# A causal 7-tap convolution and a GELU feed-forward on one core: four more seven-product blocks, a new channel order, and one operand sum made by transfers

## The chip, the cores and the metric

The kernel runs on one core of a Trainium2 chip. The metric is the device time of one execution in microseconds (us); the figure for a kernel is the median of several runs. The engines of the core are named as in the profile: PE (TensorE, matrix products; PEld is its weight load), DVE (VectorE), ACT (ScalarE), POOL (GpSimd, which here mostly issues transfers) and SP (SyncE, which issues loads and stores). Each engine works through its own instructions in the order in which they were written, and engines wait for one another through semaphores.

## The reference

The first stage is a causal convolution over the sequence with seven taps; each of eight heads has its own softmax-normalised weights, shared by the head's 24 channels. The second is a feed-forward layer with an exact GELU.

```python
batch, seq, d_model = (8, 4096, 192); kernel_size = 7; n_heads = 8
w = softmax(weight, axis=-1)                     # [8, 7]
out[b,s,h,:] = sum_k w[h,k] * x_pad[b, s+k, h, :]  # six rows of zeros ahead of each sequence
h = x @ w_in                                      # [32768,192] @ [192,2048]
g = 0.5 * h * (1.0 + erf(h * inv_sqrt2))
return (g @ w_out).astype(np.float32)             # [32768,2048] @ [2048,192]
```

(The first two lines after the sizes say in short what the reference spells out with padding, indices and an einsum.)

## The kernel before

**Tiling.** The 32768 tokens are cut into two halves that are worked on side by side, one on partitions 0 to 63 and one on partitions 64 to 127. Each half is cut into 35 blocks: six of 256 tokens, then 29 of 512 (`WS`, line 33). The 192 channels are three groups (`NP`) of 64. Before the change, group p holds channels 3r + p, r = 0 to 63, so that each partition r belongs to one head and the convolution weight of a tap is one scalar per partition (`wcol`).

**A block's way.** SP loads x (`load`, line 626, four transfers into `xin`). DVE transposes it in 32x32 squares so that channels lie on partitions (`trans`, line 777, into `xT`). POOL copies the last six columns of the block before ahead of it (`halo`, line 710). The convolution is seven taps (`conv`, line 802): the first is a multiplication, made on ACT for most blocks (`first_tap`, line 933) and on DVE otherwise; the other six are multiply-adds on DVE, the last of which writes `xc` in bf16. PE multiplies by W_in (`mm1`, line 1032) in 16 slots of 12 matmuls into the two `hp` buffers; ACT applies the GELU to each slot (line 974) into `gT`. `gT` and the other block buffers are double, indexed by the block's parity. In the next block's slots, between the pieces of its `mm1`, PE multiplies `gT` by W_out.

**The second product in two forms.** A plain block (N below; `mm2_t`, line 1129) takes 192 matmuls of 512 columns, that is 48 rounds, a round being four matmuls on the four quarters of the array. A seven-product block (S; `mm2_s`, line 1162; the list `ST`, line 72) treats part of the product as a 2x2 block matrix and uses seven products in place of eight, with sums and differences of its operands: 44 rounds. The weight sums are made once (`weights`). Per S block the following are made from `gT`: S1, S3, Dn and S4 (`st_add`, line 549; `st_dma`, line 541). S1, Dn and S4 are written to the tiles `sst`, of which there is one each; S3 is added in place in `gT`. They are made in pieces by k, the eight pairs of hidden chunks: S1 in pieces of 4, 2 and 2, Dn and S4 in halves. Before, the first two pieces of S3 are transfers that add in place, issued by POOL, and the last is a DVE addition. S1 is read by the products P5, E1 and e1, S3 by P7, Dn by P6 and S4 by P3. The order of the products in each quarter is written out by hand (`TILES`, line 388), and `ROUNDS` says how many rounds go into each slot.

**After the products of an S block** ACT copies partial sums out of PSUM (`st_copy`, line 571: p5, p1, e, u, p3, and u with a minus sign twice), DVE combines them (`st_post`, line 600: k0, k3, k4) and transposes them into `osb` (`st_evac`, line 615: ev); SP stores them (`store`, line 638). k0 waits for P7, and k4 for the end of the block's products. A bank of PSUM is handed to the next user by `release` (line 480).

**The order on DVE.** It is the convolution taps, block by block (`plan`), with the sums, combinations and transposes put between them at places listed in `AT_ST` and `at_ev`. On ACT the places of the first taps and of the copies are in `TAPS` and `AT_COPY`. On POOL, halos and transfers follow a loop over blocks (line 743).

**Before block 6** the blocks are prepared in other ways (the first two have their convolution on PE; W_in is loaded by POOL at the start, `win_in`). W_in lies in SBUF in bf16, three rows for the three channel groups on each partition, and for the upper half of the partitions with columns swapped in pairs of 256.

Of the kernel before, what the change touches and what calls it, by code (L numbers as in the profile page):

```python
# [11 lines left out]
def bass_lightweight_conv__then__act_gelu_exact_kernel(  # L12
# [39 lines left out]
    NX = 3  # L52


    DQ = D // 2

# [15 lines left out]
    ST = [m for m in range(M0 + 3, M1) if m % 2 == 1]  # L72
    K0 = {n: i for i, n in enumerate([4, 5, 6, *range(9, NB)])}
# [48 lines left out]
    with es:  # L122
# [61 lines left out]
        S_K0 = sem("S_K0")  # L184
        S_WT = sem("S_WT")
        S_ST = sem("S_ST")
# [3 lines left out]
        S_AD = [sem("S_AD%d" % q) for q in range(2)]  # L190
# [50 lines left out]
        def wait_pc(e, n, p):  # L241
# [11 lines left out]
            n: [(0, 0, 2), (0, 2, 1)] * (n not in K0) + [(k, 0, NP) for k in range(1, KS)]  # L253
            for n in range(NB)
            if n not in PC
        }
        FQ = F // 8
# [55 lines left out]
        def wait_banks(t, m, g):  # L313

            k = G0[m] + g
            if m < M0:
                if k >= 2:
                    t.wait_ge(S_EVA, k - 1)
            elif g % 2:
                t.wait_ge(S_GELU, SL0[NB] - 1 + g // 2)  # L320
            else:
                for b in LAST[g : g + 2]:
                    t.wait_ge(*release(OWNER[b], b))
# [42 lines left out]
        def evac_t(v, m, j):  # L366
# [22 lines left out]
            (0, 0): "P1 D1 e2 e1 D2 P6 P2", (1, 0): "D1 P1 P2 e2 e1 D2 P6",  # L389
            (0, 1): "P5 P7 E2 E1 P4 P3", (1, 1): "E2 P7:2 P5 P7:6 P3 E1 P4",  # L390
# [3 lines left out]
        EVENTS = []  # L394
        for (hf, cg), names in TILES.items():
            at, done = 0.0, {}
            for u in names.split():
                u, k1 = (u.split(":") + ["8"])[:2]
                k0 = done.get(u, 0)
                d = SPAN.get(u, (0, TB))[1] / TB  # L400
                for k in range(k0, min(8, k0 + int(k1))):
                    EVENTS.append((at, hf, cg, u, k))
                    at += d / 8
                    done[u] = k + 1
            assert abs(at - 5.5) < 1e-6 and all(k == 8 for k in done.values())
        EVENTS.sort(key=lambda q: (round(q[0], 4), q[1], q[2]))
        GROUP = {}
        for e, (at, hf, cg, u, k) in enumerate(EVENTS):
            name = {"D": "DE", "E": "DE", "e": "Ea"}.get(u[0], u)
            GROUP[name] = e  # L410
        DONE = {GROUP[name] for name in NE}
        SWITCH, last = {}, {}
        for e, (at, hf, cg, u, k) in enumerate(EVENTS):
            p = last.get((UNIT[u][0], cg))
            if p is not None and EVENTS[p][1] != hf:
                SWITCH[e] = p
                DONE.add(p)
            last[UNIT[u][0], cg] = e
        FIRST = {}
        for e, (at, hf, cg, u, k) in enumerate(EVENTS):  # L420
            FIRST.setdefault((UNIT[u][0], cg), e)
        DONE.discard(len(EVENTS) - 1)
        DONE = sorted(DONE)
        ROUNDS = (3, 3, 2, 3, 3, 2, 3, 3, 2, 4, 3, 3, 2, 3, 3, 2)
        assert sum(ROUNDS) == 44

        def st_done(e, m, name):
            if GROUP[name] == len(EVENTS) - 1:
                e.wait_ge(S_MM2, MMC[m + 1])
            else:  # L430
                e.wait_ge(S_ST, len(DONE) * ST.index(m) + DONE.index(GROUP[name]) + 1)

        COPIES = ("p5", "p1", "e", "u", "p3", "-u", "-g")
        AT_COPY = {
            "p5": (1, 6), "p1": (1, 8), "e": (1, 14), "u": (2, 0), "p3": (2, 2), "-u": (2, 6), "-g": (2, 10),
        }

        def ac(m, name):

            return len(COPIES) * ST.index(m) + COPIES.index(name) + 1  # L440

        POSTS = ("k0", "k3", "k4")

        def dp(m, name):

            return len(POSTS) * ST.index(m) + POSTS.index(name) + 1

        SUMS = {"S1": (0, 4, 6, 8), "S3": (6, 8), "Dn": (0, 4, 8), "S4": (0, 4, 8)}

        def sa(m, name, k):  # L450

            return (len(SUMS[name]) - 1) * ST.index(m) + [k < q for q in SUMS[name][1:]].index(True) + 1

        AT_ST = [
            (2, 1, 0, "S1", 0), (2, 1, 2, "Dn", 0), (2, 1, 4, "S4", 0), (2, 1, 6, "S1", 1),
            (2, 2, 2, "S1", 2), (2, 2, 4, "S3", 0), (2, 3, 0, "Dn", 1), (2, 4, 0, "S4", 1),
            (2, 5, 0, "k0", 0), (3, 1, 0, "ev", 2),
            (3, 6, 0, "k3", 0), (4, 1, 1, "ev", 1), (4, 1, 5, "k4", 0), (4, 2, 0, "ev", 0),
        ]

        def at_ev(n):

            if n == M0:
                return [(3, 1, 3), (3, 2, 1), (3, 2, 3)]
            return [(3, 1, 3), (3, 2, 1), (3, 2, 3)]
# [3 lines left out]
        for n in range(M0, M1):  # L469
            if n not in ST:  # L470
                SIDE += [((n + at[0], *at[1:]), "ev", n, j) for j, at in enumerate(at_ev(n))]
            else:
                SIDE += [((n + d, o, r), name, n, q) for d, o, r, name, q in AT_ST]
        SIDE.sort(key=lambda q: q[0])
        EV = {}
        for _, name, n, j in SIDE:
            if name in ("ev", "evac"):
                EV[n, j] = EVC[M0 - 1] + len(EV) + 1

        def release(m, b):  # L480
# [4 lines left out]
            if k == "X":  # L485
                return S_AC, ac(m, "p3")
# [5 lines left out]
        for m in range(M0, M1):  # L492
            for b in BK[m].values() if m in ST else BK[m]:
                REL[m, b] = release(OWNER[b], b) if b in OWNER else None
                OWNER[b] = m
# [45 lines left out]
        def st_dma(e, m, q):  # L541

            k, k1 = SUMS["S1"][q : q + 2]
            e.wait_ge(S_SA["S1"], sa(m, "S1", k))
            e.dma_start(  # L545
                quad(m, 1, 0, k, k1 - k), quad(m, 0, 0, k, k1 - k), accum_op=ALU.add
            ).then_inc(S_AD[q], 16)

        def st_add(v, m, name, q):
# [7 lines left out]
            v.wait_ge(S_GELU, SL0[m] + 2 * k1)  # L557
            if name == "S1":
                ins = v.tensor_tensor(t("S1"), quad(m, 1, 0, k, n), quad(m, 1, 1, k, n), ALU.add)  # L559
            elif name == "S3":  # L560
                v.wait_ge(S_SA["S1"], sa(m, "S1", k))
                ins = v.tensor_tensor(quad(m, 1, 0, k, n), quad(m, 0, 0, k, n), quad(m, 1, 0, k, n), ALU.add)
            elif name == "Dn":
                v.wait_ge(S_SA["S1"], sa(m, "S1", k1 - 1))
                ins = v.tensor_tensor(t("Dn"), quad(m, 0, 0, k, n), t("S1"), ALU.add)
            else:
                v.wait_ge(S_SA["Dn"], sa(m, "Dn", k1 - 1))
                ins = v.tensor_tensor(t("S4"), quad(m, 0, 1, k, n), t("Dn"), ALU.add)
            ins.then_inc(S_SA[name])

        def st_copy(a, m, name):
# [6 lines left out]
            if name[0] != "-":  # L578
                st_done(a, m, {"p5": "P5", "p1": "P1", "e": "Ea", "p3": "P3", "u": "P6"}[name])
            if name == "e":  # L580
                dst, src = bank(BK[m]["D"], UP, HA), bank(BK[m]["V"], LO, HA)
            else:
                dst, src = {
                    "p5": (p5s[UP, :], xb(UP)),
                    "p1": (gsm[LO, :], xb(LO)),
                    "u": (uu[LO, :], xb(LO)),
                    "-u": (uu[UP, :], uu[LO, :]),
                    "p3": (tq[LO, :], xb(UP)),
                    "-g": (gsm[UP, :], uu[LO, :]),
# [4 lines left out]
            if name == "p1" and i:  # L594
                a.wait_ge(S_EV, EV[ST[i - 1], 0])
            if name == "p3" and i:
                a.wait_ge(S_EV, EV[ST[i - 1], 1])
            a.activation(out=dst, in_=src, func=AF.Copy, scale=-1.0 if name[0] == "-" else 1.0).then_inc(S_AC)

        def st_post(v, m, name):  # L600
            if name == "k0":
                st_done(v, m, "P7")
                v.wait_ge(S_AC, ac(m, "p5"))
                ins = v.tensor_tensor(tq[UP, :], bank(BK[m]["Y"], UP), p5s[UP, :], ALU.subtract)
# [708 lines left out]
```

## Time and profile before

| what | us |
|---|---|
| median of 3 runs (lowest, highest) | 669.04 (668.91, 669.47) |
| the profiled execution | 667.87 |
| its span, first to last instruction | 666.1 |
| DVE convolution taps, line 827 | 282.9 of busy time, 165 instructions, plus 56.7 in 33 last taps |
| ACT gelus, line 974 | 513.0, 510 instructions |
| DVE input transposes, line 800 | 76.2, 39 instructions |
| transfers that add in place, POOL, line 545 | 26, of 512 and 256 KB |

The span is what the profile accounts for; the run's time also has what lies around it. Busy time of an engine is the time in which it had an instruction at work, and a group's mean mixes shapes unless they are told apart. A wait is the idle time of an engine ahead of an instruction, with the instruction elsewhere that ended it. The granted TensorE clock is 1.00 in every stretch. In 40 equal slices the busy tenths of DVE and ACT are 9 in most, and the DMA engines' share is 0.46 to 0.48 in the steady pairs.

### The profile page before, as it was taken

What the parts mean: (1) busy time and instruction counts of PE and PEld (TensorE: products, weight loads), DVE (VectorE), ACT (ScalarE), POOL (GpSimd) and SP (SyncE); (2) the same over time, 40 slices, a digit from 0 to 9 for tenths busy, and PEclk for the clock granted to TensorE, in tenths of its full rate; (3) what the DMA queues carried; (4) which work ended last, traced back from release to release, by engine and by line L of the source; (5) the groups of instructions that cost most, each with busy time, mean ns of one, the idle gap of its engine ahead of it and who ended that gap; (6) DMA issues with size and microseconds to landing.
All of it is one profiled execution on the core that took longest, in us unless ns stands there. A gap on an engine that the chain in (4) does not pass through costs nothing.

```text
span 666.1 us, 27567 instructions
## 1 busy us (share of the span) xinstructions
PE 661.4 (99%) x12712; PEld 516.4 (78%) x12712; DVE 600.7 (90%) x510; ACT 610.8 (92%) x720; POOL 47.6 (7%) x87
## 2 busy tenths in 40 slices
PE   8999999999999999999999999999999999999998
PEld 8999655557667787877878778787787878878787
DVE  6979999799999999999999999999999999999632
ACT  8999988889999999999999999999999999999884
POOL 7000000010000100001010010100001000010100
PEclk9999999999999999999999999999999999999999
DMA  9735334243081461905529073370824719151233
GB/s 159 165 89 130 65 69 97 72 93 79 18 197 29 107 135 34 203 7 127 114 41 201 3 163 78 62 179 2 191 50 91 151 29 192 22 118 29 56 90 97
DMA packets 137028, 63.92 MB, mean 96 GB/s; under 512 B 126800, under 2 KB 133520, under 8 KB 136912
## 3 DMA queue, kind: packets, MB, share of 16 engines
q1 hardware_dynamic: 129136, 49.37, 33.2%
q0 software_dynamic: 6656, 12.19, 10.1%
q8 instruction: 100, 1.64, 1.1%
q10 hardware_dynamic: 1120, 0.59, 0.3%
q14 instruction: 16, 0.13, 0.1%
HBM read 28.31 MB, written 25.17 MB: 80 GB/s over the span
## 4 chain that ended last, share of the span: by engine, by line
PE 99%; ACT 0%; DVE 0%; DMA 0%; issue 0%; ACTq 0%
PE hp L1066 50%; PE ob L1150 23%; PE ob L1202 18%; PE ob L1106 5%; PE ob L1258 1%; PE hp L1258 1%; PE ob L1011 0%; DMA wsb<-in_weight_dram 0%; PE ob L1066 0%; ACT dg L912 0%; DVE wcol L772 0%; ACT xc L237 0%; ACT osb L347 0%; ACT wex L899 0%; ACT xTb L269 0%
## 5 line engine op out<-in xcount | busy, mean ns | idle before, releaser
L974 ACT ACTIVATE gT<-hp 128x1024 bf16<-128x1024 f32 x510 | 513.0, 1022 | 43.0 <-PE hp L1066 35.7
L1066 PE MATMUL hp<-xc,win 64*64 64x512 bf16 (+2 forms) x6036 | 438.4, 366 | 0.2
L1066 PEld LDWEIGHTS hp<-xc,win 64*64 64x64 bf16 (+1 forms) x6036 | 247.2, 106 | 73.0 <-ACT gT L974 4.6
L827 DVE SCALAR_TENSOR_TENSOR acc<-xT,wcol,acc 128x1536 f32<-128x1536 f32 (+1 forms) x165 | 282.9, 1714 | 10.6 <-ACT acc L938 7.3
L1150 PE MATMUL ob<-gT,wot 64*64 64x512 bf16 x2880 | 205.6, 376 | 0.0
L1202 PE MATMUL ob<-gT,wot 64*64 64x512 bf16 x832 | 158.0, 376 | 0.0
L1150 PEld LDWEIGHTS ob<-gT,wot 64*64 64x64 bf16 x2880 | 112.1, 107 | 43.3
L1202 PE MATMUL ob<-gT,wst 64*64 64x512 bf16 (+2 forms) x832 | 144.0, 323 | 0.0
L1202 PE MATMUL ob<-s_S,wot 64*64 64x128 bf16 (+2 forms) x624 | 89.9, 305 | 0.0
L800 DVE STREAM_TRANSPOSE xT<-xin 128x1536 f32<-128x1536 f32 (+2 forms) x39 | 76.2, 1963 | 3.8 <-DMA xin<-in_x_dram 1.4
L1202 PEld LDWEIGHTS ob<-gT,wst 64*64 64x64 bf16 x832 | 68.5, 107 | 10.7
L1202 PEld LDWEIGHTS ob<-gT,wot 64*64 64x64 bf16 x832 | 63.9, 107 | 1.5
L938 ACT ACTIVATE acc<-xT,wcol 128x512 f32<-128x512 f32 (+1 forms) x87 | 61.2, 703 | 0.0
L827 DVE SCALAR_TENSOR_TENSOR xc<-xT,wcol,acc 128x1536 bf16<-128x1536 f32 (+1 forms) x33 | 56.7, 1720 | 0.8
L1202 PE MATMUL ob<-s_S,wst 64*64 64x512 bf16 x208 | 57.4, 376 | 0.0
L1202 PE MATMUL ob<-s_Dn,wst 64*64 64x512 bf16 x208 | 57.4, 376 | 0.0
L1202 PEld LDWEIGHTS ob<-s_S,wot 64*64 64x64 bf16 x624 | 50.2, 107 | 8.6
L545 POOL DMA_DIRECT2D gT<-gT x26 | 22.4, 861 | 318.1 <-DVE s_S L559 318.1
L1106 PE MATMUL ob<-wout,gT 64*128 64x192 bf16 x768 | 41.9, 243 | 0.0
L1106 PEld LDWEIGHTS ob<-wout,gT 64*128 64x128 bf16 x768 | 35.1, 94 | 3.3
L373 DVE STREAM_TRANSPOSE osb<-ob 128x512 f32<-128x512 f32 x45 | 31.1, 694 | 6.2 <-PE ob L1150 6.2
L559 DVE TENSOR_TENSOR s_S<-gT 128x1024 bf16<-128x1024 bf16 (+1 forms) x39 | 32.6, 837 | 1.4 <-ACT gT L974 1.3
(78 smaller groups left out, 322.6 us busy)
## 6 DMA issues: line engine op xcount, KB each, us to landing
out_dram<-osb SPq DMA_DIRECT2D x124, 192.0 KB, 3.6
xin<-in_x_dram SPq DMA_DIRECT2D x116, 192.0 KB, 4.2
gT<-gT POOLq DMA_DIRECT2D x13, 512.0 KB, 4.6
gT<-gT POOLq DMA_DIRECT2D x13, 256.0 KB, 3.3
xin<-in_x_dram SPq DMA_DIRECT2D x18, 96.0 KB, 2.5
wout<-in_moe_w_out_dram POOLq DMA_DIRECT2D x4, 192.0 KB, 4.7
win<-in_moe_w_in_dram POOLq DMA_DIRECT2D x4, 96.0 KB, 4.3
win<-in_moe_w_in_dram POOLq DMA_DIRECT2D x2, 192.0 KB, 4.5
```

What stands on the lines that cost most here:

```text
L373: v.transpose(osb_t(m, j), bank(BK[m][j])).then_inc(S_EV)
L545: e.dma_start(quad(m, 1, 0, k, k1 - k), quad(m, 0, 0, k, k1 - k), accum_op=ALU.add).then_inc(S_AD[q], 16)
L559: ins = v.tensor_tensor(t("S1"), quad(m, 1, 0, k, n), quad(m, 1, 1, k, n), ALU.add)
L800: v.transpose(out, src).then_inc(S_TR)
L827: ins = v.scalar_tensor_tensor(dst, src, wk, a, op0=ALU.mult, op1=ALU.add)
L938: a.activation(out=acc[n % 2][:, p * TB : p * TB + w], in_=ap(xT[n % 2], p * XW + HX, [[NP * XW, 128], [1, w]]), func=AF.Copy, scale=wcol[ ...
L974: a.activation(out=ap(gT[n % 2], (i % 2 * NF + i // 2) * TB if n in ST else i * c * 2 * w, dst), in_=ap(ob, 2 * TB, [[4 * TB, 128], *src[1 ...
L1066: ins = t.matmul(hbuf(u, slice(fo, fo + fw), o, w), ap(win, f1, [[NP * F, 64], [2, fw]]), xc[n % 2][r, p * TB : p * TB + w], start=(p == 0 ...
L1106: ins = t.matmul(bb[sub], gT[m % 2][r, c0 : c0 + 128], wout[r, CH[sub][i] * C : (CH[sub][i] + 1) * C], start=(ph == 0 and k == 0), stop=(p ...
L1150: ins = t.matmul(bank(BK[m][j], slice(64 * h, 64 * h + 64), w), ap(wot, 64 * hf * NF * C + CH[h][i] * C + 64 * j, [[NF * C, 64], [1, 64]]) ...
L1202: ins = t.matmul(bank(BK[m][bk], slice(64 * cg, 64 * cg + 64))[:, c0 : c0 + w], wt_, x, start=(e == mine[0]), stop=(e == mine[-1] or e in ...
L1258: ins = t.matmul(banks(m, g)[h], gT[m % 2][:, c0 : c0 + 128], wout[:, CH[h][i] * C : (CH[h][i] + 1) * C], start=(i == 0), stop=(i == NF - 1),)
```

## The change

1. **Four more seven-product blocks.** `ST` is 9, 10, 12, 13, ... 30, 31, 33: two of three blocks, 17 in place of 13.
2. **Channels in runs of eight from block 7 on.** Group p then holds channels 24h + 8p + j of each head h, j = 0 to 7. The input transpose reads runs of eight adjacent words and no longer single words at a distance of three. W_in's rows must follow: POOL loads it again in place, in four parts (`win_again`), each when block 6 has used its columns, and PE waits for each part in block 7. The halo of block 7 is made from 32 rows of x that SP loads again and DVE transposes in the new order.
3. **Sums.** S3 is wholly made by transfers. In an S block that follows an N block, the first half of Dn is too: a transfer copies `gT` into the tile, and a second adds S1. The products that read S3 stand later in the orders, of which there are now two, for an S block behind an N block and for one behind an S block.
4. **Copies.** p1 and p5 are one ACT copy of all 128 partitions (p15). The tiles `gsm` and `tq` alternate with `p5s` and `wtf` from one S block to the next.
5. **Banks** are handed over by halves of 64 partitions.
6. **Written orders.** From block 9 on DVE follows `LIST`, ACT `SLOT` and POOL `GLIST`, in which each step is named with its block. Blocks 13, 16, 19, 22, 25, 28, 31 and 34 have one third of their first tap on ACT and two thirds on DVE; the other blocks from 9 on have all of it on ACT.

```diff
-    ST = [m for m in range(M0 + 3, M1) if m % 2 == 1]
+    ST = [m for m in [9, 10, 12, 13, 15, 16, 18, 19, 21, 22, 24, 25, 27, 28, 30, 31, 33] if m < M1]
+    LIST = {
...
+        18: "Dn.1.15 ev.2.14 1 S4.1.15 ev.1.13 k0.0.15 2 S1.0.16 3 S1.1.16 4 ev.2.15 5 S1.2.16 Dn.0.16 Dn.1.16 6",
+        19: "S4.0.16 k4.0.15 t19 ev.0.15 0 S4.1.16 k0.0.16 t20 k3.0.15 1 ev.1.15 2 ev.2.16 3 4 5 k4.0.16 6",
+        20: "t21 1 S1.0.18 2 k3.0.16 3 S1.1.18 ev.0.16 4 ev.1.16 ev.0.17 ev.1.17 S1.2.18 ev.2.17 Dn.1.18 5 S4.0.18 S4.1.18 6",
+        21: "1 k0.0.18 2 t22 3 S1.0.19 S1.1.19 ev.2.18 Dn.0.19 4 S1.2.19 S4.0.19 Dn.1.19 5 k4.0.18 6",
...
+        27: "1 k0.0.24 2 t28 S1.0.25 S1.1.25 3 ev.2.24 4 S1.2.25 5 Dn.0.25 Dn.1.25 S4.0.25 k4.0.24 6",
...
+    SLOT = {
...
+        20: "0:p3.18 2:u.18 4:-g.18 6:p15.19 9:-u.18 12:f0.23 13:e.19",
+        21: "0:u.19 2:-g.19 3:p3.19 4:f1.23 6:f2.23 8:-u.19 9:f0.24 11:f1.24",
+        22: "2:f2.24 6:p15.21 12:f2.25 13:e.21",
...
+            "N": {
+                (0, 0): "P1 D1 e1 e2 D2 P6 P2", (1, 0): "D1 P1 P2 e1 e2 D2 P6",
+                (0, 1): "P5 P7:6 E1 P7 E2 P4 P3", (1, 1): "E1:4 E2:4 P7:2 P5 P7:4 P3:2 P7 P3 E2 E1 P4",
+            },
+            "S": {
+                (0, 0): "P1 D1 e2 e1 D2 P6 P2", (1, 0): "D1 P1 P2 e2 e1 D2 P6",
+                (0, 1): "P5 P7:6 E2 P7 E1 P4 P3", (1, 1): "E2 P7:2 P5 P7:4 P3:2 P7 P3 E1 P4",
+            },
...
+        ROUNDS = (3, 3, 2, 3, 3, 2, 4, 2, 2, 4, 3, 3, 2, 3, 3, 2)
...
+        BYDMA = {'N': 'S3.0 S3.1 S3.2 Dn.0', 'S': 'S3.0 S3.1 S3.2'}
...
+        def st_dma(e, m, name, q):
+
+            if name == "S3":
+                k, k1 = SUMS["S3"][q : q + 2]
+                e.wait_ge(*summed(m, "S1", k))
+                e.dma_start(
+                    quad(m, 1, 0, k, k1 - k), quad(m, 0, 0, k, k1 - k), accum_op=ALU.add
+                ).then_inc(S_AD["S3.%d" % q], 16)
+                return
+            k, k1 = SUMS["Dn"][q : q + 2]
+            d, s1 = (ap(sst[x], k * TB, [[NF // 2 * TB, 128], [1, (k1 - k) * TB]]) for x in ("Dn", "S1"))
+            if name == "cp":
+                e.wait_ge(S_GELU, SL0[m] + 2 * k1)
+                st_read(e, m, "Dn", q)
+                if ST.index(m):
+                    e.wait_ge(*summed(ST[ST.index(m) - 1], "S4", k))
+                e.dma_start(d, quad(m, 0, 0, k, k1 - k)).then_inc(S_AD["cp.%d" % q], 16)
+            else:
+                e.wait_ge(S_AD["cp.%d" % q], SUM_AT[m, "Dn", q][1])
+                e.wait_ge(*summed(m, "S1", k1 - 1))
+                e.dma_start(d, s1, accum_op=ALU.add).then_inc(S_AD["Dn.%d" % q], 16)
...
+        GLIST = (
...
+            "cp.0.18 Dn.0.18 S3.0.18 S3.1.18 S3.2.18 halo.22 S3.0.19 S3.1.19 S3.2.19 "
...
+            def win_again(k):
+                g.wait_ge(S_MM1, SL0[NR - 1] + (4, 8, 14, 16)[k])
+                c0 = 2 * FQ * (0, 2, 1, 3)[k]
+                for hf in range(2):
+                    for p in range(NP):
+                        g.dma_start(
+                            ap(win, (64 * hf * NP + p) * F + c0, [[NP * F, 64], [1, 2 * FQ]]),
+                            ap(wint, RUN * p * F + c0, [[GRP * F, 8], [F, RUN], [1, 2 * FQ]]),
+                        ).then_inc(S_WR[k], 16)
...
-                        [[TB // 32 * DQ, 128], [1, NP], [DQ, w // 32], [NP, 32]],
...
+                    if n >= NR:
+                        run = [[RUN, NP], [DQ, w // 32], [GRP, 4], [1, RUN]]
...
+                if n == NR and i in (0, 4, 8, 10):
+                    t.wait_ge(S_WR[(0, 4, 8, 10).index(i)], 32 * NP)
```

In `LIST` a bare number is a tap of the block that heads the line, `t22` the transpose of block 22, and `S1.0.19` the first piece of S1 of block 19. In `SLOT`, `12:f0.23` is the first third of block 23's first tap ahead of slot 12's GELU.

## The prediction

> **What bounds it now.** I read the page's busy shares and the chain that ended last first: the engine order is settled there.
>
> ```profile
> PE 661.4 (99%) x12712; PEld 516.4 (78%) x12712; DVE 600.7 (90%) x510; ACT 610.8 (92%) x720; POOL 47.6 (7%) x87
> ...
> PE 99%; ACT 0%; DVE 0%; DMA 0%; issue 0%; ACTq 0%
> ```
>
> PE is the whole chain; no other engine appears in it after the head. A busy PE need not be PE at its peak, so I took stretches of the steady part, each one pair of blocks (one with seven products, "S", one plain, "N").
>
> ```profile
> core 0: us, PE busy (x) PEld busy (x) DVE busy (x) ACT busy (x) POOL busy (x), PEclk, DMA share, GB/s
> 292.91:333.52 40.61, 40.61 (x791) 32.67 (x786) 39.21 (x32) 38.46 (x46) 2.55 (x4) 1.00 0.48 99
> 333.52:374.13 40.61, 40.61 (x790) 32.66 (x786) 39.21 (x32) 38.46 (x46) 2.55 (x4) 1.00 0.46 100
> ```
>
> A pair is the same 40.61 us every time, PE without a gap, DVE at 39.21 (97%), ACT at 38.46 (95%). In units of four matmuls of 512 columns on the four quarters of the array ("rounds"), a block's first product takes 48 rounds, the second 48 in N and 44 in S: 96 + 92 = 188 rounds, so a round is 40.61 / 188 = 0.2160 us, N takes 20.73 us and S 19.87. PE sets the time, with DVE 1.4 us per pair behind it. The question is therefore whether DVE and the transfers can feed more S blocks. For that I read DVE's groups by form and a piece of its timeline.
>
> ```profile
> L827 DVE SCALAR_TENSOR_TENSOR acc<-xT,wcol,acc 128x1536 f32<-128x1536 f32 x145 | 262.6, 1811 | 6.1 <-ACT acc L938 3.4
> ...
> L800 DVE STREAM_TRANSPOSE xT<-xin 128x1536 f32<-128x1536 f32 x29 | 68.6, 2369 | 2.3
> ...
> L624 DVE STREAM_TRANSPOSE osb<-tq 128x512 f32<-128x512 f32 x13 | 9.1, 702 | 0.0
> ...
> L800 DVE STREAM_TRANSPOSE xT<-xin 128x768 f32<-128x768 f32 x4 | 4.9, 1229 | 1.4 <-DMA xin<-in_x_dram 1.4
> ```
>
> ```profile
> 341.65 1.17 DVE L559 TENSOR_TENSOR s_S<-gT 128x2048 bf16<-128x2048 bf16 x1
> 342.75 0.69 DVE L624 STREAM_TRANSPOSE osb<-tq 128x512 f32<-128x512 f32 x1
> 343.38 1.17 DVE L565 TENSOR_TENSOR s_Dn<-gT,s_S 128x2048 bf16<-128x2048 bf16 x1
> ...
> 352.13 1.80 DVE L827 SCALAR_TENSOR_TENSOR acc<-xT,wcol,acc 128x1536 f32<-128x1536 f32 x1
> 353.86 1.20 DVE L565 TENSOR_TENSOR s_Dn<-gT,s_S 128x2048 bf16<-128x2048 bf16 x1
> ```
>
> The starts matter: an add of 1.17 us is followed after 1.10, a tap of 1.80 after 1.73, an output transpose after 0.63. Where a tap follows a tap directly it waits for it, and the step is 1.84. I sum steps, not durations. Last, the transfers that add in place:
>
> ```profile
> gT<-gT POOLq DMA_DIRECT2D x13, 512.0 KB, 4.6
> gT<-gT POOLq DMA_DIRECT2D x13, 256.0 KB, 3.3
> ```
>
> These are the page's medians, in us from issue to landing. Eleven of the 512 KB ones, looked up in short windows one by one, took 4.4 to 6.3, mean 4.9; this is the slowest, in the window from 464 us:
>
> ```profile
> gT<-gT POOLq DMA_DIRECT2D x1, 512.0 KB, 6.3
> ```
>
> **The change, part by part.**
>
> *PE.* 17 S blocks for 13, so four blocks lose 4 rounds each: 16 x 0.216 = **3.46 us less**. The new order of products has as many rounds. This is all that the change can gain; the rest can only take away from it.
>
> *DVE, a steady group of three (N, S, S), from the new written order.* 18 taps x 1.73 = 31.1, six of them directly behind a tap, 0.6 more; one two-thirds first tap 0.70 (the page's form of 1024 columns takes 0.77); S1 twice 1.10 + 0.59 + 0.59 = 4.6; Dn three halves (the fourth goes to a transfer) and S4 four, 7 x 1.10 = 7.7; k0, k3, k4 twice, 6 x 0.62 = 3.7; nine output transposes 5.7. S3 is gone from DVE. Sum 54.1, plus three input transposes. PE needs 20.73 + 2 x 19.87 = 60.47. The same sum for the old pair gives 39.1 against 39.21 measured, so the method holds.
>
> *The input transpose in runs of eight.* No row shows this pattern. The strided forms rise by (2369 - 1229) / 768 = 1.48 ns a column, with about 0.1 us fixed; the contiguous output transpose takes 0.70 for 512, (0.70 - 0.1) / 512 = 1.15 ns a column. Bounds: 2.37 us (no gain) and 1.70 (the taps' slope, (1811 - 1016) / 768 = 1.04 ns with the form of 768 columns, plus 0.1). I take the row of the same operation, 1.15 x 1536 + 0.1 = 1.87, a step of 1.80. Then DVE needs 54.1 + 5.4 = 59.5 of 60.47: 98%, it still fits. DVE would be the bound from a step of (60.47 - 54.1) / 3 = 2.12.
>
> [...]
>
> *ACT.* Per group 48 gelus at steps of 0.92, 7 first taps of 0.61 and two sets of copies (0.62, 0.37, 0.48, 0.62, 0.65, 0.65): 55.2 of 60.47, hidden under PE as before (91%). p1 and p5 become one copy of 128 partitions, taken at 0.62, the step of a copy of 64 partitions with as many columns; 0.72 at most, by the first tap's 128x512. It waits for the later of the two products, which ends after 16 of 44 rounds, just ahead of the slot it stands in; behind it the next gelu waits for PE anyway. Nothing.
>
> *POOL and the transfers.* Per group eight issues instead of four or five, 8 x 0.86 = 6.9 us on an engine that is 7% busy. The traffic of this queue was 10.0% of the 16 engines in a pair for 768 KB; 3 MB per 60.5 us make some 27% beside the 34% of loads and stores. What a late transfer holds up is PE at product P7. Take block 19, the second S of its group. P7 of block 18 ends after 51 rounds (11.24 us with latency); DVE then runs k0, tap, transpose, tap, S1.0: 0.61 + 1.73 + 1.80 + 1.73 + 1.18, so S1.0 ends 18.3 us into a 19.87 us block, 1.6 before the next begins. The issue follows 0.3 later (138.69 to 138.99 in the trace), and P7 of block 19 stands 15 rounds and three quarters into that block, 3.4 us. So a 512 KB transfer may take 1.6 + 3.4 - 0.3 = **4.7 us**. Blocks 22 and 31 have the same order; 25, where the 256 KB transfer goes first and one tap is left out, has 5.0; the other four have 1.5 us more or better. At the old mean of 4.9: 3 x 0.2 = **0.6 us more**. In a group's first S block POOL waits for the copy to land before it issues the addition of Dn and, behind it, S3: copy issued 11.3 us into the gelu block (eighth gelu done), two landings and 0.9, needed at 20.73 + 3.4; that holds up to 5.9 us. Bounds: at 4.4, nothing; at 6.3, below.
> *Queue order on POOL:* behind these waits stand the halos, which are needed by a tap several DVE steps after the sum that the transfer waits for; nothing, and a missed one would delay DVE, whose taps run some 10 us ahead of PE.
>
> [...]
>
> *W_in again.* 24 POOL transfers at 0.70 (the row of the first load) in block 6. The last twelve wait for its slot 14, at 81.0: issued by 89.4, landed 4.3 after the last issue, at 93.0, needed at slot 10 of block 7, 62 rounds after 83.03, at 96.4. Cover 3.4 us: nothing, and up to 2 if each issue took over 0.95. Behind them halo 9 goes out at 89.4, read at 103.
>
> *The seam at block 7.* One more transpose of 96 columns (0.1 + 96 x 0.00115 = 0.2) ahead of the halo copy; the faster transpose of block 7 gives 0.5 back, so the convolution that ends at 81.6, 1.4 before PE needs it, isn't later. SP issues four small loads ahead of one store; it idles for hundreds of us. The second copies of gsm and tq add no instruction.
>
> *Remaining slips.* With DVE at 98%, evacuations that free banks come closer to their readers; bounds 0 to 2 us by DVE's spare 1.0 per group over some eight groups that can't all be used; I take 0.3. Sum: -3.46 + 0.6 + 0.3 = **-2.6 us**. The profiled execution had a span of 666.1 in 667.87 us, the runs a median of 669.04, 1.2 above; taken from the median: **666.5**. Own range 665.2 to 667.7.
>
> **Rivals.**
> 1. *Transfers land late (slower).* For: three times the traffic on that queue, and one of 6.3 already. Against: eleven with a mean of 4.9 beside the same loads. Place: PE at P7. Price per microsecond: four blocks; 3 x (L - 4.7) + (L - 5.0) eats 3.46 at L = 5.6, and there it turns. At 6.3: 4.8 + 1.3 = 6.1, and the first S blocks, 2 x 0.4 x five of them, 4: 669.0 - 3.5 + 10.1 = **675.7**. [...] Of the rival's chance I give it 0.05, as no issue of the old kernel was held so. [...]
> 2. *DVE becomes the bound,* because the transpose gains nothing: 3 x (2.30 - 2.12) = 0.5 per group, eight groups 4.3, and the slips: about **670 to 671**. For: a fourth nested dimension in the pattern. Against: the output transposes' rate.
> 3. *The slips are 2 us rather than 0.9* (margins of a few tenths at many hand-overs): **667.6 to 668.5**, about no change.
>
> **Numbers.** Forecast 0.58, first rival 0.20, second 0.10, third 0.12. A change under 0.2% (1.3 us) can't be told from none: 667.7 to 670.4. Faster takes the forecast and a few of the third, 0.60; same takes most of the third, mild cases of the first and part of the second, 0.16; slower 0.24. The range reaches into the first rival to L = 6.0 or so, 673.
>
> **What would show it.** Right: PE still about 99% of the chain; three blocks per 60.5 us; the input transpose at 1.7 to 1.9; DVE near 98%; 512 KB transfers under 5. Wrong: PE waiting for POOL transfers at the second product (first rival); transposes above 2.2 and PE waiting for DVE taps or adds (second); a PE gap at 83 to 97 us (the reload).

## The result and the profile after

| | before | after |
|---|---|---|
| median of 19 runs each (lowest, highest), us | 669.04 (668.01, 671.16) | 671.39 (668.68, 673.69) |
| the profiled execution, us | 667.87 | 670.83 |
| its span, us | 666.1 | 669.1 |

The changed kernel takes 1.0032 of the time before, 95% interval 1.0021 to 1.0043: slower, by 2.1 us. The forecast was 2.6 us faster. The first rival happened: the transfers land late.

The page of the changed kernel, in the same order as before: span, busy shares, the software queue's share of the 16 DMA engines, and the chain that ended last.

```profile
span 669.1 us, 27895 instructions
...
PE 663.5 (99%) x12776; PEld 474.5 (71%) x12776; DVE 603.6 (90%) x537; ACT 605.5 (91%) x715; POOL 106.3 (16%) x154
...
q0 software_dynamic: 16304, 30.81, 23.8%
...
PE 93%; DMA 3%; DVE 2%; POOL 1%; issue 0%; ACT 0%; DVEq 0%; POOLq 0%
```

The busy shares look as they did, and would have told nothing. The chain tells more: PE was 99% of it and is 93%, and DMA, DVE and POOL have come in. In order of time this falls into two parts. Up to 27.3 us, at the program's start, the chain runs over a load of W_in and a load of x, with work of POOL and DVE around them (start, length, what):

```profile
3.88 5.58 DMA win<-in_moe_w_in_dram
...
13.21 5.48 DMA xin<-in_x_dram
```

Both kernels issue these loads; they are taken up under "Open" below. From there on the only transfers in the chain are two of POOL's, 12.2 us together, and the waits of PE name the place (us in total, times, longest):

```profile
PE ob L1378 <- DMA gT<-gT: 0.8, 2, 0.5
```

```profile
470.41 5.80 DMA gT<-gT
...
632.75 6.35 DMA gT<-gT
```

Line 1378 is the second product of a seven-product block, the DMA is S3's addition in place. The wait view names two stops only, 0.8 us together, so I counted all of them: a slot of a block (one gelu's worth, 16 to a block) should take (3 + its rounds of the second product) x 0.216 us, and what it takes beyond that is lost. Over blocks 7 to 34:

```
lost, us          before  after
in all              0.31   5.00
slot 2, S blocks    0.0    2.3    P7 waits for S3's first part
slot 5, 2nd S       0.0    0.9    first product pushed back by the second
slot 5, N blocks    0.0    0.55   first product waits for a gelu
block 7 starts at  83.0   85.1
```

-3.46 us of rounds, +4.69 of losses and +2.1 ahead of block 7 make +3.3, against +3.0 in the spans. The landings of the transfers issued by POOL, medians from issue to landing:

```profile
gT<-gT POOLq DMA_DIRECT2D x17, 512.0 KB, 6.0
gT<-gT POOLq DMA_DIRECT2D x34, 256.0 KB, 4.5
s_Dn<-gT POOLq DMA_DIRECT2D x9, 512.0 KB, 3.1
s_Dn<-s_S POOLq DMA_DIRECT2D x9, 512.0 KB, 6.1
```

The 512 KB addition went from 4.6 to 6.0, with single ones from 4.4 to 8.0. Two things stand beside the long ones in the profile. In blocks 12, 15, 18 and 21 S3.0 (the first piece of S3) goes out right behind the addition of Dn and shares the queue with it: it lands after 6.9 to 8.0 us there, and after 4.4 to 6.4 in the other five first S blocks of a group. In the eight microseconds around the 8.0, issued at 203.49, its own queue takes 85.4% of the engines and SP's 8.2%. The other is SP's traffic. Two windows around one landing each show the difference: the first holds a landing of 7.4 us, the second one of 4.5 (us, then busy time and instructions of each engine, the clock, the DMA engines' share, GB/s).

```profile
core 0: us, PE busy (x) PEld busy (x) DVE busy (x) ACT busy (x) POOL busy (x), PEclk, DMA share, GB/s
222.00:229.00 7.00, 7.00 (x135) 5.96 (x131) 6.93 (x6) 6.35 (x8) 1.70 (x2) 1.00 0.94 196
593.00:598.00 5.00, 5.00 (x101) 3.49 (x97) 4.97 (x6) 4.68 (x7) 2.02 (x3) 1.00 0.71 136
```

In the first, the loads and stores of SP take 54.4% of the 16 engines beside the transfer's queue at 38.5%, together 0.94; in the second that queue has the engines to itself, at 71.1%. The same 512 KB took 7.4 us in the first and 4.5 in the second.

The two parts that were in doubt did as forecast. The input transpose:

```profile
L970 DVE STREAM_TRANSPOSE xT<-xin 128x1536 f32<-128x1536 f32 x29 | 51.7, 1786 | 1.1 <-DMA xin<-in_x_dram 0.8
```

1.79 us, where 1.87 was taken. And block 7, with the reload ahead of it, loses 0.02 us.

### The profile page after: what moved, and what is told of

Same layout as the page of the kernel before. It is cut to its first block, busy times and chain, and to the rows that moved or that the text cites. A ratio compares the mean times of both kernels' runs of the same rounds, so it can differ in the third digit from the quotient of the medians.

```text
span 669.1 us, 27895 instructions
## 1 busy us (share of the span) xinstructions
PE 663.5 (99%) x12776; PEld 474.5 (71%) x12776; DVE 603.6 (90%) x537; ACT 605.5 (91%) x715; POOL 106.3 (16%) x154
## 4 chain that ended last, share of the span: by engine, by line
PE 93%; DMA 3%; DVE 2%; POOL 1%; issue 0%; ACT 0%; DVEq 0%; POOLq 0%
PE hp L1244 47%; PE ob L1378 23%; PE ob L1329 17%; PE ob L1284 4%; DMA gT<-gT 2%; DMA win<-in_moe_w_in_dram 1%; DMA xin<-in_x_dram 1%; PE ob L1434 1%; PE hp L1434 1%; DVE acc L343 1%; POOL win L827 0%; ACT gT L1151 0%; DVE xT L970 0%; POOL gT L662 0%; POOL xTb L358 0%
## 5 line engine op out<-in xcount | busy, mean ns | idle before, releaser
L1244 PEld LDWEIGHTS hp<-xc,win 64*64 64x64 bf16 (+1 forms) x6036 | 226.8, 105 | 94.6 <-ACT gT L1151 12.2
L1378 PE MATMUL ob<-gT,wst 64*64 64x512 bf16 (+2 forms) x1088 | 192.2, 323 | 1.0 <-DMA gT<-gT 0.8
L1378 PE MATMUL ob<-s_S,wot 64*64 64x384 bf16 (+2 forms) x816 | 129.9, 305 | 0.0
L1378 PEld LDWEIGHTS ob<-gT,wst 64*64 64x64 bf16 x1088 | 92.7, 107 | 15.0 <-issue 2.7
L1329 PEld LDWEIGHTS ob<-gT,wot 64*64 64x64 bf16 x2112 | 67.2, 107 | 46.7
L1378 PEld LDWEIGHTS ob<-gT,wot 64*64 64x64 bf16 x1088 | 84.5, 107 | 13.6
L1378 PE MATMUL ob<-s_S,wst 64*64 64x512 bf16 x272 | 76.4, 377 | 0.0
L1378 PE MATMUL ob<-s_Dn,wst 64*64 64x512 bf16 x272 | 75.0, 376 | 0.0
L662 POOL DMA_DIRECT2D gT<-gT x51 | 45.2, 925 | 162.9 <-DVE s_S L690 160.2
L880 POOL COPY xT<-xT 128x18 f32<-128x18 f32 x29 | 23.5, 811 | 168.0 <-DVE xc L343 149.3
L699 DVE TENSOR_TENSOR s_S<-gT,s_Dn 128x2048 bf16<-128x2048 bf16 x34 | 40.8, 1211 | 1.0 <-DMA s_Dn<-s_S 0.9
```

The costliest lines, as they stand in the source:

```text
L662: e.dma_start(quad(m, 1, 0, k, k1 - k), quad(m, 0, 0, k, k1 - k), accum_op=ALU.add).then_inc(S_AD["S3.%d" % q], 16)
L880: g.tensor_copy(dst, src).then_inc(S_HALO)
L1244: ins = t.matmul(hbuf(u, slice(fo, fo + fw), o, w), ap(win, f1, [[NP * F, 64], [2, fw]]), xc[n % 2][r, p * TB : p * TB + w], start=(p == 0 ...
L1329: ins = t.matmul(bank(BK[m][j], slice(64 * h, 64 * h + 64), w), ap(wot, 64 * hf * NF * C + CH[h][i] * C + 64 * j, [[NF * C, 64], [1, 64]]) ...
L1378: ins = t.matmul(bank(BK[m][bk], slice(64 * cg, 64 * cg + 64))[:, c0 : c0 + w], wt_, x, start=(e == mine[0]), stop=(e == mine[-1] or e in ...
```

## The experiments

Losses are counted in the profiled run as above; ratios are against runs of the kernel before on the same chip (median 668.38 for the first four, 668.59 for the next four, 668.57 for the last three).

**The changed kernel again.** 

> The changed kernel once more, for how its stages vary. In its first profile PE's slots from block 7 on ran 5.0 us over the ideal count of rounds (the old kernel 0.3), 2.3 of it in slot 2 of S blocks, and block 7 began 2.1 us later than in the old profile. Landing theory: the 512 KB additions land at a median near 6 us again and the slot-2 loss is 1.5 to 3 us, in other blocks than before, as it hangs on which loads and stores they meet. Head theory (rival): the 2.1 us ahead of block 7, where no instruction differs, are the larger part of the loss and stay in each profile; if they are chance, block 7 begins anywhere between 83 and 86 us.

670.52 us, 1.0032 (1.0020 to 1.0044): the same. Its profiled run lost more, 8.35, most of the difference in slot 2 (blocks 19, 20, 26: 1.7, 0.8, 2.3). PE's waits:

```profile
PE ob L1378 <- DMA gT<-gT: 4.0, 3, 2.1
```

The median landing of the 512 KB additions was 5.9, as the landing theory has it, and slot 2 lost more than its 1.5 to 3. So how much the landings cost varies from run to run in one kernel, 2.3 and 5.1 us; block 26 lost 1.59 more for a landing of 7.39 that took 5.80 in the first profile. Block 7 starts at 83.6 here, 85.1 there, with the same instructions.

**Rounds of their own for the second S block of a group.**

```
-ROUNDS = (3, 3, 2, 3, 3, 2, 4, 2, ...)
+ROUNDS = {"N": (3, 3, 2, 3, 3, 2, 4, 2, ...), "S": (3, 3, 2, 3, 3, 3, 3, 2, ...)}
```

> The S form behind an S block gets rounds of its own: slot 5 has three rounds and slot 6 three, so that four pieces of 384 columns end with the slot instead of two and two thirds. Form theory: the 0.12 to 0.14 us over in slot 5 of eight blocks (1.05 in all) goes, and the time falls by 1.0 us against the changed kernel. Rival: product e2 now stands 0.65 us earlier and its bank is freed by k4 on DVE with a few tenths to spare, so PE waits there instead and the time stays.

672.54 us, 1.0046 (1.0030 to 1.0061); lost 8.46. Slot 5 falls under 0.06 in blocks 11, 14, 26, 29, 32, so the 2,4 share was the loss there. But blocks 17 and 20 lose 0.6 in the same slot, up to 295.65 and 359.00 us. DVE's k4, which frees the bank of the product moved ahead, is this line in each:

```profile
294.92 0.68 DVE L754 TENSOR_TENSOR gsm<-ob,gsm 128x512 f32<-128x512 f32 x1
...
358.26 0.69 DVE L754 TENSOR_TENSOR gsm<-ob,gsm 128x512 f32<-128x512 f32 x1
```

It ends at 295.60 and 358.95, 0.05 before PE goes on: a new wait took the old one's place. Landings took 4.6 in slot 2 of blocks 19, 26 and 34 and 0.9 in slot 4 of block 23 beside it, so the run tells nothing of the net.

**Sums earlier.** S1.0 right behind k0 on DVE, ahead of the input transpose, for blocks 19, 22, 25, 28, 31; S3.0 ahead of Dn.0 or S3.1 on POOL's list.

```
-21: "1 k0.0.18 2 t22 3 S1.0.19 S1.1.19 ...
+21: "1 k0.0.18 S1.0.19 2 t22 3 S1.1.19 ...
```

> Only the written orders of DVE and POOL change: in the second S blocks 19, 22, 25, 28, 31 the first piece of S1 comes right behind k0, 1.8 to 5.2 us earlier, and S3's first transfer is issued ahead of the others (in block 25 ahead of the second piece, in blocks 12, 15, 18, 21, 33 ahead of the addition of Dn). Nothing is added or taken away. Landing theory: the loss in slot 2 falls from 2.3 us to under 0.5 and the time by 1.5 to 2.3 us against the changed kernel. Rival (DVE has no room): the taps and sums that move back by as much make PE wait elsewhere, and the time stays within 0.5.

672.55 us, 1.0062 (1.0048 to 1.0075); lost 8.80. The slot-2 loss is gone in every block, so that place was read rightly, and yet it got slower. The waits of PE, then ACT's and DVE's timeline at slot 13 of block 19 (start, length, and in brackets the idle time before it and what ended that):

```profile
PE hp L1232 <- ACT gT L1139: 4.9, 5, 1.3
```

```profile
344.82 1.02 ACT L1139 ACTIVATE gT<-hp 128x1024 bf16<-128x1024 f32 x1 [0.34 <-PE hp L1232]
346.94 0.72 ACT L1097 ACTIVATE acc<-xT,wcol 128x512 f32<-128x512 f32 x1 [1.09 <-DVE xT L958]
347.56 1.00 ACT L1139 ACTIVATE gT<-hp 128x1024 bf16<-128x1024 f32 x1
```

```profile
342.26 1.23 DVE L690 TENSOR_TENSOR s_S<-gT 128x2048 bf16<-128x2048 bf16 x1 [0.25 <-PE ob L1366]
343.40 1.81 DVE L343 SCALAR_TENSOR_TENSOR acc<-xT,wcol,acc 128x1536 f32<-128x1536 f32 x1
345.13 1.77 DVE L958 STREAM_TRANSPOSE xT<-xin 128x1536 f32<-128x1536 f32 x1
```

S1.0 at 342.26 pushed the transpose back by its 1.14. ACT's first tap of block 22 reads that transpose; ACT takes its list in order, so it stood for 1.09 us with gelus ready behind it, and PE waited for the gelu. Five blocks lose 1.1 to 1.5 us in slot 13, 5.96 in all: the wait moved from the transfer to a tap.

**Dn's first half on DVE again,** no copy and no second addition.

```
-'N': 'S3.0 S3.1 S3.2 Dn.0'
+'N': 'S3.0 S3.1 S3.2'
-20: "... S1.1.18 ev.0.16 ...
+20: "... S1.1.18 Dn.0.18 ev.0.16 ...
```

> The first half of Dn goes back to DVE in all S blocks: 18 transfers of 512 KB less, from 3 to 2 MB per group of three blocks, and 1.1 us per group more on DVE. Landing theory: the 512 KB additions land at a median of 4.8 to 5.3 us instead of 6.0, the slot-2 loss of blocks 13, 19 and 34 (1.0 us) goes, that of 20, 26, 29 shrinks, and the time falls by 1 to 2 us. Rival (DVE has no room): DVE comes to about 60 of 60.5 us, and PE waits in new places for taps, sums or freed banks; same or slower by 1 to 3 us.

673.48 us, 1.0069 (1.0056 to 1.0081); lost 8.64. The transfers did come sooner:

```profile
gT<-gT POOLq DMA_DIRECT2D x17, 512.0 KB, 5.1
gT<-gT POOLq DMA_DIRECT2D x34, 256.0 KB, 3.5
```

and slot 2 of blocks 13, 19 and 34 falls to nothing. But DVE has no room for one more add per group in this order: slot 13 of blocks 22, 28 and 31 loses 1.8, slot 0 of block 19 0.8, and slot 2 of block 26, where S3.1 goes ahead of S3.0, still 1.9. So moving Dn to transfers shortens DVE's list, and its price is the landings; whether an order exists in which DVE keeps Dn, was not tried.

**ACT's tap three slots later,** on top of the early sums.

```
-19: "6:p15.18 12:f2.22 13:e.18"
+19: "6:p15.18 13:e.18 15:f2.22"
```

> The early sums of e3_early, and ScalarE's five first taps of blocks 22, 25, 28, 31 and 34 moved from slot 12 to slot 15 of their blocks. In e3_early the wait for S3.0's landing was gone (slot 2 at 0 in all blocks), but slot 13 of blocks 19, 22, 25, 28 and 31 lost 5.96 us, since S1.0 had pushed the input transposes back 1.18 us and ScalarE stood at its first tap with gelus behind it. Theory (that standing tap alone gave the gain back): slot 13 falls to under 0.3 us in all, slot 2 stays under 0.3, the loss over blocks 7 to 34 falls from 8.80 to 2 to 3 us (slot 5: 1.0 in second-S blocks, 0.5 in N blocks), and the time lands 5 to 6 us under e3_early, at 667 to 668.5, ratio 0.997 to 1.000. Rival (VectorE has no room for any advance: what is moved ahead pushes something else late): slot 13 falls, but another slot of the same blocks takes over most of 6 us, ratio 1.003 or more.

667.89 us, 0.9992 (0.9984 to 1.0001); lost 4.04. Slot 13 and slot 2 are at nothing: they were two separate waits, and the standing tap had given the gain back. The loss is above the 2 to 3 us expected: the tap now crowds the copies of the next block (slot 1 of blocks 20, 23, 26, 29, 32: 1.0), and 0.4 go in slot 6 of block 16, where PE waits for an evacuation by DVE.

**With the rounds of five blocks changed as well.** 

> e5_early_taps with 3, 3 rounds in place of 2, 4 in slots 5 and 6 of blocks 11, 14, 26, 29 and 32 alone, the five where e2_rounds showed slot 5 at under 0.06 us. Theory (the 2,4 share breaks the second form's E2 pieces, and the share costs 0.13 us a block where the bank is free): 0.13 x 5 = 0.6 us under e5_early_taps, the loss over blocks 7 to 34 at 1.5 to 2.4 us, ratio 0.996 to 0.999. Rival (in these blocks too the earlier matmuls only find the next wait, k4 or the gelu): same loss as e5_early_taps within 0.2 us.

668.91 us, 1.0002 (0.9993 to 1.0011); lost 4.48. Slot 5 of blocks 11, 29 and 32 falls to nothing, blocks 14 and 26 lose 0.3 and 0.9 there, waiting for DVE's k4. The loss is 0.4 above the run before instead of 0.6 below it: the rival, in kind.

**The kernel before with the runs of eight and the reload alone.** 

> The kernel before with the runs of eight from block 7 on and W_in's reload alone, 14 seven-product blocks as before. Theory (TensorE sets the time, the transpose is not on its path, the reload hides under the 3.4 us landings): input transposes at 1.79 in place of 2.37 us, VectorE 28 x 0.58 = 16 us less busy, loss over blocks 7 to 34 at 0.2 to 0.5 us as before (0.31), ratio 0.9985 to 1.0015. Rival (the reload's 24 transfers or the rearranged layout cost by themselves, and part of the 2 us ahead of block 7 in the changed kernel comes from them): block 7 starts at 85 us or later or loses over 0.5 us in blocks 7 and 8, ratio 1.002 or more.

668.41 us, 0.9994 (0.9986 to 1.0003); lost 0.34, block 7 starts at 83.4. (It has 13 seven-product blocks, as before; the 14 in the expectation is a slip.)

```profile
PE 662.7 (99%) x12712; PEld 515.9 (77%) x12712; DVE 584.6 (88%) x511; ACT 611.1 (92%) x720; POOL 64.3 (10%) x111
```

```profile
L818 DVE STREAM_TRANSPOSE xT<-xin 128x1536 f32<-128x1536 f32 x29 | 51.9, 1793 | 2.3
```

DVE is 16 us less busy (600.7 before) and the time is the same: PE sets it, the reload is free, and the new order by itself gains nothing.

**The changed kernel with the old channel order.**

```
-RUN, NR = GRP // NP, 7
+RUN, NR = GRP // NP, 1000
```

> The changed kernel with the channels left in their old order throughout, so transposes as before (2.37 us) and no reload; 17 seven-product blocks and everything else as changed. Theory (VectorE is at its limit in a group of three blocks: 54.1 + 3 x 1.79 = 59.5 of TensorE's 60.47 us, so with 2.37 it needs 61.2 and becomes the bound): 0.7 us a group over 8 groups, and 0.58 us later at each wait on a transposed block: loss over blocks 7 to 34 up from 5.0 to 10 to 14 us, 676 to 681 us, ratio 1.011 to 1.017. Rival (VectorE's 90% leaves room on the average, and the losses are landings only): loss as in the changed kernel, ratio 1.003 to 1.005.

677.35 us, 1.0128 (1.0111 to 1.0144); lost 14.1. One group of three, first in the changed kernel and then here:

```profile
391.63:452.35 60.72, 60.72 (x1188) 40.78 (x1184) 59.67 (x51) 56.82 (x68) 9.45 (x10) 1.00 0.63 135
```

```profile
391.10:452.70 61.60, 61.40 (x1188) 46.15 (x1184) 61.20 (x51) 57.02 (x68) 9.41 (x10) 1.00 0.63 131
```

DVE goes from 59.67 of 60.72 us to 61.20 of 61.60: in this group it is the bound now, and the group is 0.9 longer. The seven groups from block 10 to block 30 are 0.1 to 0.95 longer, 3.5 us together. The last, blocks 31 to 33, is 5.7 longer, and there DVE itself stands: it waits for a load of x ahead of a transpose (its longest wait of this kind, below), ACT's tap waits for the transpose and PE for the gelu behind the tap, and slot 13 of block 31 loses 2.8. After that stop the granted clock of PE is 0.58 from 598 to 602 us, 1.00 behind it (0.997 in the mean of that execution), and slots 14 and 15 lose 1.7. So the loss comes near the 10 to 14 us expected in part by chance.

```profile
DVE xT L970 <- DMA xin<-in_x_dram: 4.3, 4, 2.4
```

**Only the order on the queue.** S3.0 ahead of Dn.0 (blocks 12, 18, 33) or S3.1 (25) on POOL; S1.0 of blocks 19 and 22 ahead of tap 3 but behind the transpose.

```
-cp.0.18 Dn.0.18 S3.0.18 ... S3.1.25 S3.0.25 ... Dn.0.33 S3.1.33 S3.0.33
+cp.0.18 S3.0.18 Dn.0.18 ... S3.0.25 S3.1.25 ... S3.0.33 Dn.0.33 S3.1.33
-21: "1 k0.0.18 2 t22 3 S1.0.19 S1.1.19 ...
+21: "1 k0.0.18 2 t22 S1.0.19 3 S1.1.19 ...
```

> The changed kernel with the landings helped and no transpose pushed back: on GpSimd's queue S3.0 goes ahead of Dn.0 for blocks 12, 18 and 33 and ahead of S3.1 for block 25; on VectorE S1.0 of blocks 19 and 22 goes ahead of tap 3 but stays behind the transpose. ScalarE's taps stay at slot 12. Theory (the slot-2 loss is S3.0's landing and is set by its place in the queue; the slot-13 loss of e3_early came from the moved transposes alone): slot 2 falls from 2.3 to under 0.7 us, slot 13 stays under 0.3 us, loss over blocks 7 to 34 from 5.0 to 3.0 to 3.7 us, ratio 0.998 to 1.001, level with e5_early_taps or under it by 0.5 us. Rival (landings are long wherever a transfer stands in the queue, at 6 us, and Dn.0 or S3.1 is late instead): slot 2 or the slots of P6 and P7's later part lose 1.5 us or more, ratio 1.002 to 1.004 as in the changed kernel.

667.44 us, 0.9981 (0.9971 to 0.9991); lost 3.37. Slot 2 is down to 0.2 us, and the landings are hardly shorter:

```profile
gT<-gT POOLq DMA_DIRECT2D x17, 512.0 KB, 5.7
gT<-gT POOLq DMA_DIRECT2D x34, 256.0 KB, 4.6
```

What changed is when the urgent transfer starts. POOL's timeline at block 18's sums, in the changed kernel and then here (L673 the copy, L677 the addition of Dn, L662 S3):

```profile
321.00 0.56 POOL L673 DMA_DIRECT2D s_Dn<-gT  x1 [3.45 <-ACT gT L1151]
326.18 0.85 POOL L677 DMA_DIRECT2D s_Dn<-s_S  x1 [4.62 <-DMA s_Dn<-gT]
326.72 2.07 POOL L662 DMA_DIRECT2D gT<-gT  x2
```

```profile
319.88 0.56 POOL L673 DMA_DIRECT2D s_Dn<-gT  x1 [3.45 <-ACT gT L1139]
321.18 0.85 POOL L662 DMA_DIRECT2D gT<-gT  x1 [0.74 <-DVE s_S L690]
324.72 0.86 POOL L677 DMA_DIRECT2D s_Dn<-s_S  x1 [2.69 <-DMA s_Dn<-gT]
```

S3.0 stood behind POOL's wait for the copy, 4.62 us; ahead of it, it goes out 1.3 us after the copy instead of 5.7. One stop of 0.8 in slot 13 (block 31) is left, the same tap ahead of its transpose.

**And the rounds of blocks 11, 29 and 32.** 

> e9_queue_order with 3, 3 rounds in slots 5 and 6 of blocks 11, 29 and 32 alone, the three where both e2_rounds and e6_early_taps_rounds lost under 0.05 us in slot 5. Theory (in these blocks the 2,4 share is the loss): 3 x 0.13 = 0.4 us less loss than e9_queue_order, slot 5 of the three under 0.05. Rival (the loss moves to another slot of the same blocks): the same loss as e9_queue_order within 0.15 us.

667.02 us, 0.9979 (0.9968 to 0.9989); lost 1.98, with slot 5 of the three at nothing. Its page:

```profile
span 664.3 us, 27895 instructions
...
PE 660.1 (99%) x12776; PEld 466.9 (70%) x12776; DVE 603.9 (91%) x537; ACT 604.9 (91%) x715; POOL 105.2 (16%) x154
...
PE 98%; DMA 1%; POOL 1%; DVE 0%; issue 0%; ACT 0%; POOLq 0%
```

This one beats both kernels, the changed one by 0.5% (0.9979 / 1.0032). Against the ninth run it gains too little to tell (the intervals overlap); of the 1.4 us between the two counts, slot 5 of the three blocks makes 0.4, the rest is block 31's stop, 0.8, and chance.

**ACT's copies spread in blocks 15, 18, 21, 27,** on top of the tenth run, whose rounds it keeps, though its expectation names the ninth.

```
-18: "0:u.16 2:p3.16 3:-g.16 4:f1.20 6:f2.20 ..."
+18: "0:u.16 2:p3.16 4:f1.20 5:-g.16 6:f2.20 ..."
```

> e9_queue_order with ScalarE's copies and taps of blocks 15, 18, 21 and 27 spread: one of them moved from slots 2 to 4 to slot 5, so that no three stand in neighbouring slots. Theory (the slot-5 loss of the N blocks, 0.09 to 0.22 us each, 0.55 in all, is the gelu pushed back by the cluster ahead of it): slot 5 of these blocks falls to under 0.05 each, 0.4 to 0.5 us less loss, nothing elsewhere over 0.1. Rival (ScalarE is at 91% and has no slot to spare): the loss goes to slot 6 or 7 of the same blocks, same loss as e9_queue_order within 0.15 us.

670.87 us, 1.0035 (1.0024 to 1.0045); lost 6.39, against the tenth run's 1.98. Slot 5 of those blocks does fall to nothing. But a copy frees a bank and a tap feeds DVE, and PE waits for DVE in new places:

```profile
PE ob L1366 <- DVE osb L461: 1.5, 1, 1.5
...
PE ob L1366 <- DVE s_S L690: 0.8, 1, 0.8
```

Slot 0 of block 19 loses 1.7 (an output transpose comes late), slot 2 of block 22 1.1 (a piece of S1). The loss went elsewhere and grew, as the rival says in kind, though in other blocks than it named.

**All runs together.** What the count foretells, the loss less 0.31 less 3.46 us (without the 3.46 for the kernel with 13 blocks as before), against the measured ratio times 668.5:

```
run                   lost   count  measured
changed kernel        5.00   +1.2    +2.1
the same again        8.35   +4.6    +2.1
rounds                8.46   +4.7    +3.1
sums earlier          8.80   +5.0    +4.1
Dn on DVE             8.64   +4.9    +4.6
sums and taps         4.04   +0.3    -0.5
sums, taps, rounds    4.48   +0.7    +0.1
before, runs of eight 0.34    0.0    -0.4
old channel order    14.1   +10.3    +8.6
queue order           3.37   -0.4    -1.3
queue, rounds         1.98   -1.8    -1.4
queue, spread         6.39   +2.6    +2.3
```

One profiled run stands against a median of several, so 1 to 2 us of difference are to be expected. The farthest, the second row, had its profile in the slowest of its 12 runs, 672.69 against their median of 670.52. Against the span of its own profile each count does better: with the time at which block 7 starts in that profile added (less the 83.0 of the kernel before), it comes out 0.0 to 0.5 us above the measured difference of the spans in all twelve rows. So the count and the start of block 7 hold nearly all of the time that moves.

## Why the prediction was wrong

**The failed step is the transfers' term,** "At the old mean of 4.9: 3 x 0.2 = 0.6 us more". The place was right, PE at P7, and so was the allowance: block 20 loses 0.37 us at a landing of 4.87 of block 19's sum, block 32 nothing at 4.45 of block 31's, block 26 0.69 at 5.80 of block 25's, so 4.5 to 5.1 may pass where 4.7 and 5.0 were worked out. The size was wrong, on two counts. The length was carried over from a queue with 10% of the engines to one with 24%: 6.0 instead of 4.6 in the median, 6.05 instead of the 4.9 taken in the mean. And in blocks called safe ("1.5 us more or better", "that holds up to 5.9") landings of 6.4 to 8.0 overran it: blocks 13, 19, 29 and 34 lose 1.2 of the 2.3 us. In three of them, blocks 13, 19 and 34, S3.0 also stood behind Dn's half on the queue; the ninth run took that away, and the loss with it. In the second profile the term was 5.1. The first rival named the reason, three times the traffic, and the place. Its own formula gives 4.9 us at L = 6.0 and 1.0 more for the first S blocks, 671.5, close to the 671.4 measured (the prediction's last lines put that L at 673, which the formula doesn't give). The agreement is luck: the landings cost 2.3 and 5.1 us and not 5.9, and the next two points and the start of block 7 made the rest.

**Second, "The new order of products has as many rounds".** As many, but the 2,4 share of slots 5 and 6 does not fit the second S form: 0.12 to 0.14 us in seven of the eight blocks, 0.9 in all. The round count is a bound, not a time.

**Third, "behind it the next gelu waits for PE anyway. Nothing".** True of a single copy, not where three of ACT's extras, the copy -g among them, stand in slots 2 to 4: 0.09 to 0.22 us in blocks 15, 18, 21 and 27, 0.55 in all. (Blocks 12 and 30 have three extras without -g there and lose nothing.)

**The remaining slips** were put at 0.3 us; the two losses just named are of that kind, 1.5 together, near the third rival's 2 us. Its sum alone would still have been no slower than before. Slips and landings together were more than the 3.46 us that the change can gain.

**What held.** The rounds' 3.46 us: the tenth run lost 1.67 more than the kernel before and measured 1.4 us less, where 3.46 less 1.67 is 1.8. The transpose's 1.87 against 1.79 (its slope, 0.60 us over 512 columns, is 1.17 ns and not 1.15, which would have made it 1.90). DVE's group of 59.5: 59.67. DVE near its bound without the runs of eight: 3.5 us over seven groups in the eighth run, where the second rival had 0.5 a group. The reload at nothing. The 0.05 within the first rival's chance is for issues that are held back. Neither profile shows one: a POOL issue of S3 that stands alone took 840 to 930 ns, as before (847 to 942), and what grew is the time after the issue, 4.6 to 6.0 us in the median.

**Open:** block 7 starts anywhere from 83.3 to 85.2 us in the profiles of the changed kernel and its variants that share the instructions ahead of it, and at 83.0 to 83.4 in the three kernels that lack the 17 blocks, the reload or both. Where a late start comes from can be read: in the first 55 us DVE, ACT and POOL have the same instructions in the same order in all thirteen profiles, but the fourth load of x that POOL issues lands between 15.5 and 17.1 us where block 7 starts by 83.6, and between 17.9 and 18.7 where it starts at 84.3 to 85.1. (In the one profile left, of the run with the sums earlier, PE stood still for 1.3 us up to 14.7.) Why these loads differ, whether the change has a part in it, and whether the mean moved by some tenths, isn't settled.

## What to carry to other kernels

A transfer's landing time belongs to the load it was measured under (here 4.6 us in the median with the queue at 10% of the engines, 6.0 at 24%): if a change multiplies a queue's traffic, price the landings at their slowest, and count how many places have less allowance than that. Where DVE and ACT are at 98 and 94% of a group that PE fills, the order of the lists decides: put the transfer that is waited for first on its queue, and before moving anything ahead on one engine ask which in-order engine stands waiting for what was pushed back. Busy shares hide all this; the time of each slot against its own ideal shows it.

## What was not expected of the hardware

The same 512 KB moved as a plain copy landed after 3.1 us in the median (2.8 to 4.9), as an addition in place after 6.0 (4.4 to 8.0); one addition that was issued 0.55 us behind another (203.49) took 8.0, and one with SP's queue at 3.0% of the engines and nothing else of its own queue for the first 3.1 us (410.33) took 4.4.

GpSimd's halo copies of 18 columns took 527 ns in the mean before, 621 with the runs of eight alone, 718 with the 17 blocks alone and 811 with both, though not one of them changed. The timelines show where the time goes. Two copies of the kernel before, and what DVE did at the time:

```profile
348.31 0.96 POOL L723 COPY xT<-xT 128x18 f32<-128x18 f32 x1
...
364.15 0.20 POOL L723 COPY xT<-xT 128x18 f32<-128x18 f32 x1 [14.88 <-DVE xc L827]
```

```profile
347.41 1.80 DVE L827 SCALAR_TENSOR_TENSOR acc<-xT,wcol,acc 128x1536 f32<-128x1536 f32 x1
...
364.18 2.39 DVE L800 STREAM_TRANSPOSE xT<-xin 128x1536 f32<-128x1536 f32 x1
```

Beside a transpose, or with DVE idle, a copy takes 0.20 to 0.24 us in both profiles, but for two of the changed kernel that start in the last 0.4 us of an output transpose, ahead of an add (1.54 us) and of a tap (2.13). One that starts beside a multiply-add tap ends 0.05 to 0.06 us after the tap, with 0.77 to 1.67 us of it left at the start; the same shows beside the adds that make Dn and S4 (1.13 us with 1.07 of the add left, in the changed kernel). So the mean depends on which of DVE's instructions the copies happen to meet.

In the eighth run PE stood for 2.4 us and had a granted clock of 0.58 in the four us that followed, 1.00 before and behind; its mean was 0.997. The instructions ahead of block 7, the same in ten profiles, were through at 83.3 us in one and at 85.2 in another.
